# Batch 1's turned u accumulated in PSUM, and the steps of its mixer placed later

## The chip, the core and the metric

The kernel runs on one core of one Trainium2 chip. The metric is the device time of one execution in microseconds. Five runs of the kernel before gave 222.54 to 223.18 us, with a median of 222.9 us. One more look at the same program is a profile, from which all rows below come. TensorE is called PE in the rows, VectorE DVE, ScalarE ACT, GpSimd POOL and the queue of SyncE SP or SPq; PEld is TensorE loading weights.

## What is computed

Four batches of 768 positions and 512 channels (8 heads of 64). First a retention layer, whose output x is the input of a mixer with a low-rank product over positions and an MLP over channels:

```python
for t in range(S):
    state = gamma * state + k[t] (outer) v[t]      # per batch and head
    y[t] = scale * q[t] @ state
x = y as (batch, position, 512)
u = x + (x.T @ U @ V).T                            # U: 768x32, V: 32x768
out = u + relu(u @ w_ch1) @ w_ch2                  # 512 -> 2048 -> 512
```

## The kernel before, in words

**Retention in chunks.** Each batch has 6 chunks of 128 positions, in 3 pairs. For a chunk, `state` (line 482) adds k x v to a running state in one PSUM bank and ScalarE copies it out; `score_one` (521) multiplies turned k by turned q into two "s" banks (line 506), and VectorE screens them with the causal mask (line 516); `mix` (532) multiplies q by the incoming state (line 540) and the screened scores by v (line 545) into the "o" bank, which ScalarE copies to x (line 548). Before that, `prep_keys` (280) scales q and k and casts v on GpSimd, and for batch 1 `turn_pe` (461) turns q and k on TensorE into the one "qk" bank (line 465); ScalarE copies the result out, for q in two steps (`q_order`, 453), for k as kT. For batches 2 and 3 the turns are DMA transposes.

**The mixer.** `lr_open` and `lr_proj` (554, 559) project x by U; the result `pc` is a small tile copied by VectorE. `lr_grow` (571) multiplies it by V into four banks, one for each 128 channels (line 576), and `lr_add` (580) adds these to x in place on VectorE (line 582): the tile x is then the plain u. `lr_expand` (586) is both. The MLP wants u turned, as `uT`. Batch 0 gets its first 512 positions of uT without the plain u: `x_turn` (861) turns x by multiplying it with an identity matrix into four PSUM banks (line 865), four 512-column products of V and pc are accumulated into the same banks (line 929), and ScalarE and VectorE copy them out by turns. Batch 1 has its plain u made first and then turned by TensorE's transposes, in pairs of 128 channels (`lr_turn_pair`, 599, into fp16 "s" banks); batches 2 and 3 use DMA transposes (line 609). The last two chunks of a batch are done at the start of its own MLP (`first`, lines 935 and 945: `lr_expand` and, for batches 0 to 2, `lr_turn_pe` of chunks 4 and 5).

**The MLP and the weave.** `mlp_pieces` (761) gives a list of TensorE pieces with their costs: 16 wide up pieces (512 positions, line 772), 16 narrow ones (256 positions), each with a relu on ScalarE or VectorE, and down pieces. In batch 0 the down product is plain: 24 pieces of four 512-column matmuls (line 823), four to an output chunk, with an addition of u on VectorE at the end of each chunk (line 828). In batches 1 to 3 it takes seven half products in place of eight (`down_pairs`, 652), for which VectorE makes sums of w2 beforehand (`w2_sums`, 632: four subtractions of 512 columns for each two blocks of w2; line 617 is where a `part` runs them).

**What sets the order.** The order is written out by hand. `weave` (837) walks through the pieces of batch b-1's MLP and adds up their costs; every other step (retention of batch b, its turns, its mixer, the w2 sums) has a mark, a share of the MLP's total cost, and is issued before the first piece that reaches it. So a mark's meaning is a place in the instruction queue of each engine, and each engine works through its queue in order. For batch 1 the marks come from a list `at`, one for each chunk:

```python
at = [0.475, 0.58, 0.64, 0.695, 0.75, 0.802]
lag = [0.01, 0.035, 0.065]
...
steps = [(state, at[i] + lag[0]),
         (score_one, at[i] + lag[1] - 0.015 * (i == 5)),
         (mix, at[i] + lag[2] + more)]
```

The total cost of batch 0's MLP in the weave's own units is 41.5, of which the 24 down pieces begin at half.

**Banks.** PSUM has 8 banks here, given out by name: "mlp" has three (four from batch 1's MLP on, when "qk" joins), "s" two, "o", "qk" and "st" one each. A step that takes a bank waits until the last reader of its former content is done.

**Loads.** SP issues all loads in order through a ring of 16 tiles, each refilled when GpSimd has read it. After the last load of batch 2, SP's queue holds that batch's six DMA transposes, the six stores of batch 0 and the loads of batch 3.

Of the kernel before, what the change touches and what calls it, by code (L numbers as in the profile page):

```python
# [11 lines left out]
fp16 = mybir.dt.float16  # L12
# [6 lines left out]
def kernel(  # L19
# [11 lines left out]
    nc = tc.nc  # L31
# [40 lines left out]
    def bank(tag, dtype=fp32):  # L72
        n_bank[0] += 1
        ring = RINGS[tag]
        ring.append(ring.pop(0))
        return psum.tile([P, 2048 // (4 if dtype == fp32 else 2)], dtype,
                         tag=f"bank{ring[-1]}", name=f"{tag}_{n_bank[0]}",
                         bufs=1)

    def four(t):  # L80
        return t.rearrange("p (n m) -> p n m", n=4)

    def evac(eng, dst, src):
        if eng == "A":
            nc.scalar.activation(dst, src, AF.Copy)  # L85
        else:
            nc.vector.tensor_copy(out=dst, in_=src)
# [508 lines left out]
        evac("A", uTs[b][:, ds(j0, 2)].rearrange("p j c t -> p (j c) t"),  # L596
             tp.rearrange("p (n t) -> p n t", t=P))

    def lr_turn_pair(b, c0, eng):
        tp = bank("s", fp16)  # L600
        for c in range(c0, c0 + 2):
            for j in range(NLO):
                nc.tensor.transpose(tp[:, ts(NLO * (c - c0) + j, P)],
                                    us[b][:, j, ts(c, P)], ident16)
        evac(eng, uTs[b][:, :NLO, ds(c0, 2)].rearrange("p j c t -> p c j t"),
             tp.rearrange("p (c j t) -> p c j t", c=2, j=NLO))

    def lr_turn(b, j):
        nc.sync.dma_start_transpose(  # L609
            out=uTs[b][:, ds(j, 2)].rearrange("p j c t -> p (j c) t"),  # L610
# [247 lines left out]

    xT = {}

    def x_turn(c, j0):
        if j0 == 0:
            xT[c] = bank("mlp" if c < 3 else "o")
        for j in range(j0, j0 + 2):
            nc.tensor.matmul(xT[c][:, ts(j, P)], xs[0][:, j, ts(c, P)], ident16,
                             start=(j == 0), stop=False, skip_group_check=True)

    def prep_pair(nm, sc, engs):
        for hh in range(2):
# [55 lines left out]
        x_turn(c, 0)  # L925
        x_turn(c, 2)
    idle_bank[0] = bank("s")
    for c in range(NCB):
        nc.tensor.matmul(xT[c][:, :LO], pcs[0][ds(RK * c, RK)],
                         V4[ds(RK * c, RK), :LO], start=False, stop=True,  # L930
                         skip_group_check=True)
    for c in range(NCB):
        evac("AD"[c % 2], uTs[0][:, :NLO, c], four(xT[c]))
    keep_busy(3)
    first = [part(lr_expand, 0, 4, 2), part(lr_turn_pe, 0, 4),
             part(lr_expand, 0, 0, 4)]
# [4 lines left out]
    for b in range(1, B + 1):  # L941
        tracks = []
        if b > 1:
            old = b - 1 < SEVEN
            first = [part(lr_expand, b - 1, 4, 2, "qk" if old else "st"),
                     part(lr_turn_pe, b - 1, 4, "qk" if old else "o")
                     if b < 3 else part(lr_turn, b - 1, 4)]
            if not old:
                RINGS["mlp"] = [6, 0, 1, 2]
        tracks.append((first, *((0.02, 0.2), (0.02, 0.14), (0.0, 0.06),  # L950
                                (0.0, 0.03))[b - 1]))
        if b < B:
            if b == 1:
                at = [0.475, 0.58, 0.64, 0.695, 0.75, 0.802]
                lag = [0.01, 0.035, 0.065]
                for sc in range(NSC):
                    keys = pair(b, sc)
                    c0, c1 = 2 * sc, 2 * sc + 1
                    if sc:
                        tracks.append(([part(prep_keys, b, keys[:AHEAD])],  # L960
                                       at[c0] - 0.1, 1))
                    tracks.append(([part(prep_keys, b, keys[AHEAD:])],
                                   at[c1] - 0.1, 1))
                    for f, d in ((part(turn_pe, "q", b, sc),
                                  at[c0] - (0.04, 0.03, 0.032)[sc]),
                                 (part(turn_pe, "k", b, sc, (0,)),
                                  at[c0] + (0.0, 0.014, 0.014)[sc]),
                                 (part(turn_pe, "k", b, sc, (1,)), at[c1])):
                        tracks.append(([f], d, d))
                for sc in range(NSC):  # L970
                    tracks.append(([part(prep_keys, 2, pair(2, sc))],
                                   at[-1] - 0.05 + 0.03 * sc, 1))
                for i in range(2 * NSC):
                    tracks.append(([part(turn_dma, "kq"[i % 2], 2, i // 2)],
                                   0.84, 0.84))
                for f, d in zip(w2_sums(0) + w2_sums(2),
                                (0.515, 0.53, 0.55, 0.6, 0.65, 0.685, 0.71,
                                 0.745)):
                    tracks.append(([f], d, d))
            else:  # L980
                at = [(0.205, 0.06)[b - 2] + (0.074, 0.1)[b - 2] * i
                      for i in range(NCK)]
                lag = [0.0, 0.04, 0.1]
                two = [(0.25, 0.395, 0.595), (0.1, 0.27, 0.44)][b - 2]
                if b == 2:
                    for _ in range(RING):
                        feed_one(False)
                    steps = [(0.01 + 0.022 * i, f)
                             for i, f in enumerate(w2_sums(4) + w2_sums(6))]
                    for sc in range(NSC):  # L990
                        steps.append((0.57 + 0.08 * sc,
                                      part(prep_keys, 3, pair(3, sc))))
                        for nm in "kq":
                            if not sc:
                                steps.append((0.64, part(turn_dma, nm, 3, sc)))
                else:
                    steps = [(0.08, part(turn_dma, nm, 3, sc))
                             for sc in (1, 2) for nm in "kq"]
                for d, f in steps:
                    tracks.append(([f], d, d))  # L1000
            if b > 1:
                for sc in range(NSC):
                    d = two[sc] - (0.04, 0.05, 0.08 if b == 2 else 0.05)[sc]
                    tracks.append(([lambda b=b, sc=sc: q_order(
                        b, sc, live["q", b, sc])], d, d))
            for i in range(NCK):
                more = 0.012 if b == 1 and i in (0, 2) else 0.0
                if b == 2 and i > 3:
                    p = two[2] + 0.062 * (i - 4)
                    steps = [(state, p - 0.035), (score_one, p),  # L1010
                             (mix, p + 0.075)]
                elif b > 1:
                    p = two[i // 2]
                    steps = [(state, p + (-0.035, 0.02)[i % 2]),
                             (mix, p + (0.08, 0.12)[i % 2])]
                    if i % 2 == 0:
                        steps.append((score_two, p))
                else:
# [3 lines that stand above are left out]
                for f, d in steps:  # L1022
                    tracks.append(([part(f, b, i)], d, d))
            t = at[-1] + lag[2] if b == 1 else two[-1] + 0.122
            if b == 1:
                tracks += [([part(lr_open, b), part(lr_proj, b)], t + 0.02,
                            t + 0.02),
                           ([part(lr_expand, b, 0, 4)], t + 0.04, t + 0.04),
                           ([part(lr_turn_pair, b, 0, "A"),
                             part(lr_turn_pair, b, 2, "D")], t + 0.08, t + 0.12)]  # L1030
            else:
                for fs, d in (([part(lr_open, b), part(lr_proj, b)],
                                (0.042, 0.03)[b - 2]),
                              ([part(lr_grow, b, 0, 4, "st")], 0.065),
                              ([part(lr_add, b, 0, 4, (0,))], 0.065),
                              ([part(lr_add, b, 0, 4, (1,))], 0.075),
                              ([part(lr_add, b, 0, 4, (2,))], 0.1),
                              ([part(lr_add, b, 0, 4, (3,))], 0.12),
                              ([part(lr_turn, b, 0)], 0.14),
                              ([part(lr_turn, b, 2)], 0.141)):  # L1040
                    tracks.append((fs, t + d, t + d))
        weave(b == 1, mlp_pieces(b - 1), *tracks)
# [29 lines left out]
```

## Time and profile before

| what | before |
|---|---|
| median of 5 runs | 222.9 us |
| the profiled execution, its own time | 222.68 us |
| its span, first to last instruction | 220.9 us |
| TensorE busy, share of the span | 212.0 us, 96% |
| VectorE busy | 140.0 us, 63% |
| ScalarE busy | 92.9 us, 42% |
| GpSimd busy | 81.9 us, 37% |
| the first up piece of batch 0's MLP starts | 28.32 us |
| its first down piece starts | 51.31 us |
| the first up piece of batch 1's MLP starts | 84.54 us |
| the first up piece of batch 2's MLP starts | 132.66 us |
| GpSimd's last conversion for batch 2 ends | 87.43 us |

How to read it: the span is what the profile's rows cover, and 1.8 us of the execution's own time lie around it. Matmuls are pipelined, so the rows of TensorE overlap, and the time that a step costs is read from the start of its row to the start of the next one. A row's bracket at its end tells how long the engine stood idle before it and which instruction released it.

### The profile page before, as it was taken

The page shows a single profiled execution, that of the slowest core. Times are in us where ns is not written, and L with a number is a line of the kernel's source. Part 1 is how long each engine was busy: PE and PEld are TensorE (multiplying, and loading weights), DVE is VectorE, ACT ScalarE, POOL GpSimd, SP SyncE. Part 2 cuts the span into 40 slices and gives each one's busy share as a digit, 9 for nine tenths or more (in the row PEclk, how much of TensorE's full clock was granted, in tenths as well). Part 3 has the DMA queues.
Part 4 walks back from the last instruction along what each step waited for, and adds up shares of the span by engine and source line. Part 5 has one row for each costly group of instructions (what it writes and reads, how often), then busy time and mean ns, then how long its engine had stood idle before and what let it go on. Part 6 is the DMA issues. An engine that isn't in the chain of part 4 may idle for free. (4 is left out here: it accounts for less than half of the span.)

```text
span 220.9 us, 5513 instructions
## 1 busy us (share of the span) xinstructions
PE 212.0 (96%) x2235; PEld 148.1 (67%) x2235; DVE 140.0 (63%) x302; ACT 92.9 (42%) x191; POOL 81.9 (37%) x121
## 2 busy tenths in 40 slices
PE   7979999999998999999999989999999999999994
PEld 2768754596554554667788774767788856668884
DVE  7478666235554558599686854598977442867443
ACT  3357654475556214676911005768510035551000
POOL 5456868986987868000059930000000000000000
PEclk9999999999999999999999999999999999999999
DMA  5999999999999999999999578900003541000043
GB/s 163 301 292 268 235 358 283 369 363 217 237 238 233 243 223 223 184 331 252 231 231 178 169 166 189 123 1 3 0 3 71 190 145 24 3 1 0 10 160 119
DMA packets 84489, 38.82 MB, mean 176 GB/s; under 512 B 58384, under 2 KB 77552, under 8 KB 84464
## 3 DMA queue, kind: packets, MB, share of 16 engines
q1 hardware_dynamic: 83456, 36.84, 69.9%
q10 hardware_dynamic: 1008, 1.64, 2.1%
q8 instruction: 17, 0.28, 0.6%
q14 instruction: 8, 0.07, 0.1%
HBM read 27.46 MB, written 6.29 MB: 153 GB/s over the span
## 5 line engine op out<-in xcount | busy, mean ns | idle before, releaser
L772 PE MATMUL mlp<-uT,w1b 128*128 128x512 f16 (+1 forms) x512 | 88.9, 326 | 0.8 <-DMA uT<-x 0.8
L782 ACT ACTIVATE gT<-mlp 128x512 f16<-128x512 f32 (+1 forms) x98 | 47.2, 490 | 61.9 <-PE mlp L772 59.8
L772 PEld LDWEIGHTS <-w1b 128*128 128x128 f16 x512 | 48.2, 98 | 30.9 <-issue 1.1
L780 DVE TENSOR_SCALAR gT<-mlp 128x512 f16<-128x512 f32 (+1 forms) x30 | 16.7, 557 | 28.5 <-PE mlp L772 27.9
L664 PEld LDWEIGHTS <-gT 128*128 128x128 f16 x288 | 27.7, 98 | 3.3
L823 PE MATMUL mlp<-w2b,gT 128*128 128x512 f16 x96 | 24.2, 380 | 0.0
L516 DVE TENSOR_TENSOR a<-s,mask 128x512 bf16<-128x512 f32 x26 | 16.7, 683 | 8.3 <-PE s L506 8.2
L306 POOL TENSOR_TENSOR kd<-in,gk 128x512 bf16<-128x512 f32 x18 | 19.4, 1088 | 5.5 <-DMA in<-in_k_dram 4.9
L664 PEld LDWEIGHTS <-gS 128*128 128x128 f16 x200 | 19.2, 98 | 2.6
L85 ACT ACTIVATE x<-o 128x512 f16<-128x512 f32 x20 | 11.9, 596 | 17.5 <-PE o L545 17.1
L306 POOL TENSOR_TENSOR qd<-in,gq 128x512 bf16<-128x512 f32 x18 | 18.8, 1063 | 0.0
L664 PE MATMUL A<-w2t,gT 128*128 128x256 f16 x144 | 18.4, 273 | 0.0
L85 ACT ACTIVATE state<-st 64x256 bf16<-64x256 f32 x40 | 15.0, 375 | 7.3 <-PE st L490 3.5
L823 PEld LDWEIGHTS <-gT 128*128 128x128 f16 x96 | 8.2, 98 | 7.2
L304 POOL CAST vd<-in 128x512 bf16<-128x512 f32 x18 | 10.9, 618 | 1.7 <-DMA in<-in_v_dram 1.2
L340 POOL CAST w1b<-in 128x512 f16<-128x512 f32 x16 | 9.7, 613 | 2.8 <-DMA in<-in_moe_w_ch_dram 2.3
L346 POOL CAST w2b<-in 128x512 f16<-128x512 f32 x16 | 9.6, 614 | 1.5 <-DMA in<-in_moe_w_ch_dram 0.8
L617 POOL COPY gate<-gT 128x1 f16<-128x1 f16 x1 | 0.2, 190 | 25.4 <-DVE gT L617 25.4
L664 PE MATMUL B<-w2b,gT 128*128 128x256 f16 x72 | 9.3, 273 | 0.0
L582 DVE TENSOR_TENSOR x<-s,x 128x256 f16<-128x256 f32 (+1 forms) x16 | 8.1, 548 | 1.2 <-issue 0.7
L664 PE MATMUL A<-w2t,gS 128*128 128x256 f16 x72 | 8.9, 273 | 0.0
L664 PE MATMUL A<-w2b,gT 128*128 128x256 f16 x72 | 8.8, 272 | 0.0
(151 smaller groups left out, 288.5 us busy)
## 6 DMA issues: line engine op xcount, KB each, us to landing
in<-in_moe_w_ch_dram SPq DMA_DIRECT2D x32, 256.0 KB, 5.5
in<-in_k_dram SPq DMA_DIRECT2D x24, 256.0 KB, 5.5
in<-in_q_dram SPq DMA_DIRECT2D x24, 256.0 KB, 4.7
in<-in_v_dram SPq DMA_DIRECT2D x24, 256.0 KB, 5.3
out_dram<-o SPq DMA_DIRECT2D x16, 256.0 KB, 2.3
out_dram<-o ACTq DMA_DIRECT2D x6, 256.0 KB, 2.1
out_dram<-o SPq DMA_DIRECT2D x3, 128.0 KB, 1.7
Uf<-in_moe_U_dram SPq DMA_DIRECT2D x1, 96.0 KB, 5.9
```

The lines of the kernel that those rows point to most:

```text
L85: nc.scalar.activation(dst, src, AF.Copy)
L304: nc.gpsimd.tensor_copy(out=t, in_=src)
L306: nc.gpsimd.tensor_tensor(t, src, g, op=ALU.mult)
L340: nc.gpsimd.tensor_copy(out=w1b[:, c, ts(mb, 512)], in_=take("w1", mb, c))
L346: nc.gpsimd.tensor_copy(out=w2b[:, m], in_=take("w2", m))
L516: nc.vector.tensor_tensor(a, four(sp[i]), causal(mask), op=ALU.mult)
L582: nc.vector.tensor_tensor(us[b][:, ds(j0, nj), ts(c, P)], four(grown[b][c])[:, :nj], xs[b][:, ds(j0, nj), ts(c, P)], op=ALU.add)
L664: nc.tensor.matmul(acc[key, i], lhs[:, m, ts(i, P)], rhs[:, m], start=(fresh and m == 0), stop=(m == NH - 1), skip_group_check=True)
L772: nc.tensor.matmul(g_p[:, :sz], w1b[:, c, ts(m, P)], uTs[b][:, ds(j, nj), c], start=(c == 0), stop=(c == NCB - 1))
L780: nc.vector.tensor_relu(gT[:, m, ds(lo, sz)], g_p[:, :sz])
L782: nc.scalar.activation(gT[:, m, ds(lo, sz)], g_p[:, :sz], AF.Relu)
L823: nc.tensor.matmul(ch, gT[:, m, ts(j, P)], w2b[:, m], start=(m == 0), stop=(m == NM - 1))
```

## The change

- Batch 1's first 512 positions are turned as batch 0's are: `x_turn` now takes a batch and a bank, and the four-product part with its copies is a function, `grow_turned`. The four banks are "qk", "st" and both "s". The first two are turned before the projection, the other two behind it. `lr_turn_pair` is gone, and so is the making of batch 1's plain u for these positions in MLP 0.
- That plain u is made in MLP 1 instead: its 16 products (`lr_grow`) at 0.1 of that MLP, its four VectorE additions (`lr_add`) at 0.1 to 0.166.
- The w2 sums of blocks 4 and 5 (and of their partners 12 and 13), four VectorE subtractions, move from MLP 1 to MLP 0, and the other eight there get other places.
- The list `at` of batch 1 is later by 0.015 to 0.033; the q turns lie 0.042 ahead of their chunk, the k turns of a pair's first chunk at its mark. The marks for preparing batch 2's k, q and v stay where they were.
- GpSimd's and SP's queues hold the same instructions in the same order as before. TensorE has 4 more matmuls.

```diff
@@ -596,15 +596,6 @@
         evac("A", uTs[b][:, ds(j0, 2)].rearrange("p j c t -> p (j c) t"),
              tp.rearrange("p (n t) -> p n t", t=P))
 
-    def lr_turn_pair(b, c0, eng):
-        tp = bank("s", fp16)
-        for c in range(c0, c0 + 2):
-            for j in range(NLO):
-                nc.tensor.transpose(tp[:, ts(NLO * (c - c0) + j, P)],
-                                    us[b][:, j, ts(c, P)], ident16)
-        evac(eng, uTs[b][:, :NLO, ds(c0, 2)].rearrange("p j c t -> p c j t"),
-             tp.rearrange("p (c j t) -> p c j t", c=2, j=NLO))
-
     def lr_turn(b, j):
         nc.sync.dma_start_transpose(
             out=uTs[b][:, ds(j, 2)].rearrange("p j c t -> p (j c) t"),
@@ -858,12 +849,20 @@
 
     xT = {}
 
-    def x_turn(c, j0):
+    def x_turn(c, j0, b=0, tag=None):
         if j0 == 0:
-            xT[c] = bank("mlp" if c < 3 else "o")
+            xT[c] = bank(tag or ("mlp" if c < 3 else "o"))
         for j in range(j0, j0 + 2):
-            nc.tensor.matmul(xT[c][:, ts(j, P)], xs[0][:, j, ts(c, P)], ident16,
+            nc.tensor.matmul(xT[c][:, ts(j, P)], xs[b][:, j, ts(c, P)], ident16,
                              start=(j == 0), stop=False, skip_group_check=True)
+
+    def grow_turned(b):
+        for c in range(NCB):
+            nc.tensor.matmul(xT[c][:, :LO], pcs[b][ds(RK * c, RK)],
+                             V4[ds(RK * c, RK), :LO], start=False, stop=True,
+                             skip_group_check=True)
+        for c in range(NCB):
+            evac("AD"[c % 2], uTs[b][:, :NLO, c], four(xT[c]))
 
     def prep_pair(nm, sc, engs):
         for hh in range(2):
@@ -925,12 +924,7 @@
         x_turn(c, 0)
         x_turn(c, 2)
     idle_bank[0] = bank("s")
-    for c in range(NCB):
-        nc.tensor.matmul(xT[c][:, :LO], pcs[0][ds(RK * c, RK)],
-                         V4[ds(RK * c, RK), :LO], start=False, stop=True,
-                         skip_group_check=True)
-    for c in range(NCB):
-        evac("AD"[c % 2], uTs[0][:, :NLO, c], four(xT[c]))
+    grow_turned(0)
     keep_busy(3)
     first = [part(lr_expand, 0, 4, 2), part(lr_turn_pe, 0, 4),
              part(lr_expand, 0, 0, 4)]
@@ -951,7 +945,7 @@
                                 (0.0, 0.03))[b - 1]))
         if b < B:
             if b == 1:
-                at = [0.475, 0.58, 0.64, 0.695, 0.75, 0.802]
+                at = [0.49, 0.6, 0.665, 0.725, 0.783, 0.835]
                 lag = [0.01, 0.035, 0.065]
                 for sc in range(NSC):
                     keys = pair(b, sc)
@@ -962,20 +956,20 @@
                     tracks.append(([part(prep_keys, b, keys[AHEAD:])],
                                    at[c1] - 0.1, 1))
                     for f, d in ((part(turn_pe, "q", b, sc),
-                                  at[c0] - (0.04, 0.03, 0.032)[sc]),
+                                  at[c0] - 0.042),
                                  (part(turn_pe, "k", b, sc, (0,)),
-                                  at[c0] + (0.0, 0.014, 0.014)[sc]),
+                                  at[c0]),
                                  (part(turn_pe, "k", b, sc, (1,)), at[c1])):
                         tracks.append(([f], d, d))
                 for sc in range(NSC):
                     tracks.append(([part(prep_keys, 2, pair(2, sc))],
-                                   at[-1] - 0.05 + 0.03 * sc, 1))
+                                   0.752 + 0.03 * sc, 1))
                 for i in range(2 * NSC):
                     tracks.append(([part(turn_dma, "kq"[i % 2], 2, i // 2)],
                                    0.84, 0.84))
-                for f, d in zip(w2_sums(0) + w2_sums(2),
-                                (0.515, 0.53, 0.55, 0.6, 0.65, 0.685, 0.71,
-                                 0.745)):
+                for f, d in zip(w2_sums(0) + w2_sums(2) + w2_sums(4),
+                                (0.53, 0.545, 0.56, 0.59, 0.64, 0.655, 0.71,
+                                 0.725, 0.765, 0.79, 0.865, 0.885)):
                     tracks.append(([f], d, d))
             else:
                 at = [(0.205, 0.06)[b - 2] + (0.074, 0.1)[b - 2] * i
@@ -986,7 +980,10 @@
                     for _ in range(RING):
                         feed_one(False)
                     steps = [(0.01 + 0.022 * i, f)
-                             for i, f in enumerate(w2_sums(4) + w2_sums(6))]
+                             for i, f in enumerate(w2_sums(6))]
+                    steps.append((0.1, part(lr_grow, 1, 0, 4, "st")))
+                    steps += [(0.1 + 0.022 * c, part(lr_add, 1, 0, 4, (c,)))
+                              for c in range(NCB)]
                     for sc in range(NSC):
                         steps.append((0.57 + 0.08 * sc,
                                       part(prep_keys, 3, pair(3, sc))))
@@ -1023,11 +1020,14 @@
                     tracks.append(([part(f, b, i)], d, d))
             t = at[-1] + lag[2] if b == 1 else two[-1] + 0.122
             if b == 1:
-                tracks += [([part(lr_open, b), part(lr_proj, b)], t + 0.02,
-                            t + 0.02),
-                           ([part(lr_expand, b, 0, 4)], t + 0.04, t + 0.04),
-                           ([part(lr_turn_pair, b, 0, "A"),
-                             part(lr_turn_pair, b, 2, "D")], t + 0.08, t + 0.12)]
+                turns = [part(x_turn, c, j0, b, tag)
+                         for c, tag in enumerate(("qk", "st", "s", "s"))
+                         for j0 in (0, 2)]
+                for fs, d in ((turns[:4], t + 0.006),
+                              ([part(lr_open, b), part(lr_proj, b)], t + 0.022),
+                              (turns[4:], t + 0.023),
+                              ([part(grow_turned, b)], t + 0.044)):
+                    tracks.append((fs, d, d))
             else:
                 for fs, d in (([part(lr_open, b), part(lr_proj, b)],
                                 (0.042, 0.03)[b - 2]),
```

## The prediction

> **What bounds the kernel now.** I read the page first, then the chain of waits, then TensorE's timeline from 27 us to 139 us, adding up what each step should take and looking for the steps that took longer.
>
> ```profile
> PE   7979999999998999999999989999999999999994
> PEclk9999999999999999999999999999999999999999
> ...
> PE 39%; DMA 2%; SPq 1%; DVE 0%; issue 0%
> ```
>
> TensorE is busy in every slice at full clock and carries the chain that ended last (the two small shares, DMA and SP's queue, are one wait at batch 2's turn). So this is a TensorE-order kernel: its time changes by TensorE work added or taken away, and by the holes in its queue. The other engines count only where they make such a hole. The holes of the first MLP, where the change works, are seen in TensorE's timeline:
>
> ```profile
> 57.61 0.27 PE L465 MATMUL qk<-ident,qd 128*128 128x128 bf16 x2
> 58.33 0.51 PE L465 MATMUL qk<-ident,qd 128*128 128x128 bf16 x6 [0.45 <-POOL qd L306]
> ...
> 60.20 0.64 PE L545 MATMUL o<-vd,a 128*128 128x64 bf16 x8
> 60.67 1.03 PE L823 MATMUL mlp<-w2b,gT 128*128 128x512 f16 x4
> ...
> 61.98 1.03 PE L823 MATMUL mlp<-w2b,gT 128*128 128x512 f16 x4
> 63.41 0.40 PE L506 MATMUL s<-qO,kT 64*128 64x128 bf16 x8 [0.41 <-ACT kT L85]
> ...
> 69.24 0.29 PE L545 MATMUL o<-vd,a 128*128 128x64 bf16 x4
> 69.84 0.29 PE L545 MATMUL o<-vd,a 128*128 128x64 bf16 x4 [0.31 <-DVE a L516]
> 69.97 0.39 PE L490 MATMUL st<-vd,kd 128*128 128x128 bf16 x4
> ...
> 70.41 1.03 PE L823 MATMUL mlp<-w2b,gT 128*128 128x512 f16 x4
> 72.10 0.40 PE L506 MATMUL s<-qO,kT 64*128 64x128 bf16 x8 [0.66 <-ACT kT L85]
> ```
>
> Ends overlap in these rows, so I go from start to start. Undisturbed prices, from neighbouring rows: a down piece (4 matmuls) 0.87, a wide up piece 0.87, a narrow one 0.44, a q turn 0.45, a k turn or state step 0.22, a score step 0.33, a mix 0.23 (first) or 0.45, and 0.09 more when tiles change from 128 rows to 64 or 32. Against these the holes are:
> - q turn of pair 1: 57.61 to 58.77 = 1.16, less 0.44: 0.72, for POOL's q.
> - mix 1: 0.47, less 0.23: 0.24 (no releaser printed; its screens started at 59.20 and took 1.29).
> - score 2: 1.43 before it, less 0.96: 0.47, for ScalarE's kT.
> - mix 3: 0.73, less 0.23: 0.50, for VectorE's screen.
> - score 4: 1.69, less 0.96: 0.73, for ScalarE's kT.
>
> Together 2.66 us. From 75 us to batch 2's turn at 131 us I find no hole.
>
> **The change part by part.**
>
> *TensorE's work for batch 1's u.* Out go 16 products L576 (0.33) and 16 transposes (L603, 0.45 per 8 from 81.92 to 82.37, so 0.90). In come 16 identity matmuls and four 512-column products; the same code for batch 0 shows both: 8 in 0.45 (26.48 to 26.93), and 27.25 to 27.58 = 0.33 for the four. So the tail of MLP 0 costs TensorE the same, with the same two tile switches. The plain u's 16 products come again in MLP 1: +0.33, +0.09 for a switch = **+0.42**.
> Here a rule has to be weighed. The Trainium skill ("TensorE: Matmul & The Clock Gate", Part 4: PE-mode transpose) puts a 128x128 transpose at about 275 ns in a kernel and says that the clock does not rise for it. Taken as issue time, swapping 16 transposes for matmuls would then be worth 16 x (275 - 56) ns = 3.5 us. The rows contradict that: L603 transposes and L865 identity matmuls both last 219 ns and follow each other every 56 ns at granted clock 1.00. I take the rows: the swap is worth nothing.
>
> *The chain at the end of MLP 0.* Before: projection 78.43, products 79.85, four VectorE additions 80.56 to 83.0, transposes, two copies of 1.02 and 0.69, up at 84.54, all hidden under down pieces. After: turned x, projection, grown product, four copies, two on each engine. By batch 0's rows from the grown product to the last copy's end it is 29.00 - 27.25 = 1.75. Two down pieces and the product itself make 0.33 + 1.74 = 2.07 before the up pieces, so it is hidden by 0.3; without one of these pieces it would cost 0.55. The chain is shorter, and that is what lets all steps be placed about 0.03 of the MLP later; by itself it saves nothing.
>
> *The steps moved.* I lay the new order on the old timeline. Narrow up pieces begin at 43.46. Twelve of them instead of ten bring the first q turn to 48.67 (was 47.80). Its copies qO on ScalarE end 2.0 after its start as before (48.44 + 1.34 against 47.80), at 50.65; the relu of the next piece is queued behind them until 50.9, and the fourth piece needs its bank (at 50.42). That is a new hole of 0.5; the first down piece is then at 51.6 (was 51.31). Behind it queue kT and the first score, all of TensorE's.
> This hole costs nothing, for the q turn of pair 1 keeps its place behind six down pieces. It would start at 58.1 and must wait for POOL's q, whose second half begins on TensorE at 58.33. It ends at 58.77 as before, POOL being fed by DMA and its queue, like SP's, keeping its order. Without that cover the 0.5 would be paid in full.
> From 58.77 on: a down piece now precedes score 1 (59.73), and down piece and k turn lie between score and mix. Mix 1 starts 61.15; its second screen is ready at 60.06 + 1.39 = 61.45 and used at 61.49: hole gone. Score 2 is at 63.66; its kT was turned at 60.93 and copied by 61.9, with no qO and no state copy in front: gone. q turn 2 is at 66.16 (q ready at 64.66). Score 3 is at 68.02, its screen done at 69.74, used at 69.78 in mix 3: gone, by 0.04. Its o bank needs x(2), behind two state copies and two qO copies, about 69.0; mix 3 starts 69.44. Score 4 is at 71.93, its kT turned at 69.22 and ready by 70.2: gone. Mix 4 starts 73.35, but screen 4 stands behind an output addition (71.95 to 72.6): ready 73.85, wanted 73.69: a new **0.2**. Score 5 at 75.0, mix 5 at 77.1, turned x at 77.5, projection at 78.9, grown product at 80.8, MLP 1 at about 82.8 against 84.54.
> As a sum: 0.24 + 0.47 + 0.50 + 0.73 = 1.94 removed, 0.2 new: **-1.74**.
>
> *VectorE's load.* Four w2 differences leave MLP 1 for MLP 0 (0.42 each, 1.7), four additions (0.68 each, 2.6) go the other way. The first lie in VectorE's idle time before scores, except for what POOL does to them. The skill speaks against placing them there: "GPSIMD Engine Reference", section 1, Specifications, says that POOL's SBUF interfaces are shared and contended by VectorE instructions with two SBUF inputs, as these are. The rows: 14 of 16 at 0.41 to 0.44, but 1.13 at 56.24 and 1.06 at 85.35, under POOL's q, and POOL's 2.04 us pairs stretched to 2.2 to 2.3. By the rule all four are slowed: +0.7 each on VectorE, and POOL's q for pair 1 could come 0.2 later, on the path. By most rows it is nothing. A gain is excluded, for nothing of this load leaves POOL's busy time. I take 0 and keep +0.2.
>
> *The plain u in MLP 1.* Its products stand one up piece behind the turn of the last two chunks, and want bank o, which ScalarE must empty first. In the rows of before:
>
> ```profile
> 88.32 0.61 PE L594 MATMUL o<-ident,x 128*128 128x128 f16 x8
> ...
> 88.97 1.02 ACT L85 ACTIVATE uT<-o 128x1024 f16<-128x1024 f16 x1 [0.71 <-PE o L594]
> ```
>
> From turn to empty bank 1.67; turn, one piece and switch take 0.45 + 0.87 + 0.09 = 1.41: a new wait of 0.26, say **+0.3** with the semaphore. Nothing in the trace has this wait; bounds 0 (a gain is excluded, since products were not there) and 1.0 (a relu in front of the copy, 0.6 more). Behind it stand the up pieces, and ScalarE and VectorE waiting for these; all shift together. The four additions end some 0.3 before the state step of batch 2 wants bank st.
>
> *The rest.* The wait at 132.66 (0.79) follows TensorE's own projection by a fixed chain and moves with it. From there nothing changes.
>
> Sum: -1.74 + 0.42 + 0.3 = **-1.0 us**. The profiled execution took 222.68 (span 220.9), so 221.7; the median of the runs is 222.9, so **221.9**.
>
> **The rivals.**
> - *The holes only move (wash).* ScalarE's queue around 66 to 69 us holds 0.77 + 1.34 + 0.60 of copies and I left 0.4 before mix 3; mix 3's screen has 0.04. Against it: the long gaps from k turn to score. If two of the four holes come back (mean 0.49), -1.0 + 0.97: about 222.8.
> - *Slower: ScalarE's queue hands its wait on.* Place: the kT copies ahead of scores 2 and 4. If a kT copy waits behind qO, state and x copies still, all of the 1.94 stays and 0.72 of MLP 1 is added: 223.6. It decides from kT being ready more than 1.7 us later than I have it (scores at 63.66 and 71.93 against copies ending 61.9 and 70.2). The unhurried ScalarE queue (idle 1.68 before kT at 65.04) speaks against it.
> - *More than I say.* Bank o is empty in time and mix 4 waits not: -1.0 - 0.5, and q of pair 1 arriving 0.2 earlier: about 221.2.
> - *That the stalls belonged to data, not order:* POOL's q at 58.27 is the only one, and I keep it.
>
> **How the numbers follow.** My forecast 0.60 (221.4 to 222.4), the larger gain 0.10, the wash 0.16, slower 0.14. A measurement here can tell about 0.2% (0.45 us) from no change. Faster by more: 0.60 + 0.10 = 0.70; the wash 0.16; slower 0.14. The range 221.2 to 223.0 takes in forecast, wash and half of the larger gain, with +0.2 for POOL and +0.7 for bank o inside it.
>
> **What would show it.** MLP 1's first up product near 82.8, no wait for kT, the q turn of pair 1 still waiting for POOL until about 58.3, a hole of 0.5 before it for ScalarE, one of 0.2 at mix 4, one of 0.3 before the plain u's products. I am wrong if scores 2 and 4 or mix 3 still wait, if q of pair 1 is later than 58.5, or if the up pieces of MLP 1 wait for a uT copy.

## The result and the profile after

The changed kernel takes 222.05 us, the median of 43 runs (221.40 to 222.68), the kernel before 222.4 us (80 runs, 221.62 to 223.37; its first five had given 222.9). The ratio is 0.9982 with a 95% interval of 0.9975 to 0.9990, so the change saves 0.4 us (0.2 to 0.6), where 1.0 was forecast, with a chance of 0.70 for a gain above 0.45. The profiled execution took 222.24 us with a span of 220.5.

In the changed kernel's line numbers L763 is an up piece, L814 a down piece of MLP 0, L771 and L773 are relus, and L608 stands for the w2 sums (L617 before). On its page, TensorE and its clock look as before, and TensorE carries 92% of the chain that ended last (in the kernel before, the chain began at the wait for batch 2's turn, at 126 us):

```profile
PE   7989999999999999999999989999999999999994
PEclk9999999999999999999999999999999999999999
...
PE 92%; DVE 3%; ACT 3%; issue 1%; ACTq 0%
```

TensorE's timeline at the places of the old holes (columns: start, duration, engine, line, operation, operands, count, and in brackets the idle time before it):

```profile
49.84 1.47 PE L763 MATMUL mlp<-uT,w1b 128*128 128x256 f16 x12
51.67 0.60 PE L763 MATMUL mlp<-uT,w1b 128*128 128x256 f16 x4 [0.35 <-ACT gT L773]
...
58.84 0.61 PE L465 MATMUL qk<-ident,qd 128*128 128x128 bf16 x8
59.29 1.03 PE L814 MATMUL mlp<-w2b,gT 128*128 128x512 f16 x4
...
61.90 0.42 PE L545 MATMUL o<-vd,a 128*128 128x64 bf16 x8
62.15 1.03 PE L814 MATMUL mlp<-w2b,gT 128*128 128x512 f16 x4
63.02 0.39 PE L490 MATMUL st<-vd,kd 128*128 128x128 bf16 x4
63.24 1.03 PE L814 MATMUL mlp<-w2b,gT 128*128 128x512 f16 x4
64.20 0.40 PE L506 MATMUL s<-qO,kT 64*128 64x128 bf16 x8
...
70.23 0.42 PE L545 MATMUL o<-vd,a 128*128 128x64 bf16 x8
70.48 1.03 PE L814 MATMUL mlp<-w2b,gT 128*128 128x512 f16 x4
71.34 0.39 PE L490 MATMUL st<-vd,kd 128*128 128x128 bf16 x4
71.57 1.03 PE L814 MATMUL mlp<-w2b,gT 128*128 128x512 f16 x4
72.53 0.40 PE L506 MATMUL s<-qO,kT 64*128 64x128 bf16 x8
...
74.18 0.69 PE L545 MATMUL o<-vd,a 128*128 128x64 bf16 x8
74.70 1.03 PE L814 MATMUL mlp<-w2b,gT 128*128 128x512 f16 x4
```

Mixes 1 and 3 now take 0.25 from start to start, and scores 2 and 4 follow their down piece after 0.96: the four holes are gone. New are the hole before the piece at 51.67 (1.83 for three pieces worth 1.31: 0.52) and that of mix 4 (0.52 less 0.23: 0.29). One thing is not as forecast: the q turn of pair 1 at 58.84 doesn't wait for POOL; it takes 0.45.

In MLP 1 the plain u's products stop for bank o, which ScalarE empties (its copy ends at 88.97):

```profile
87.30 0.61 PE L594 MATMUL o<-ident,x 128*128 128x128 f16 x8
87.75 1.03 PE L763 MATMUL mlp<-uT,w1b 128*128 128x512 f16 x4
87.95 1.02 ACT L85 ACTIVATE uT<-o 128x1024 f16<-128x1024 f16 x1 [0.71 <-PE o L594]
88.71 0.23 PE L576 MATMUL s<-pc,V 32*128 32x128 f16 x2
89.03 0.21 PE L576 MATMUL o<-pc,V 32*128 32x128 f16 x1
```

From the first product at 88.71 to the first that writes bank o at 89.03 are 0.32 us.

For comparing profiles I measure stages by the starts of TensorE's rows: "opening" is the start of the first up piece of MLP 0, "MLP 0" runs from there to the first up piece of MLP 1, "up 1" from there to its first down piece, and "q turn" is how long the q turn of pair 1 waited: what it took beyond 0.44, or beyond 0.53 where a score follows it (before, c0, e4, e8), since the change to tiles of 64 rows costs 0.09.

| kernel | opening | MLP 0 | up 1 | q turn | median of runs | ratio to before |
|---|---|---|---|---|---|---|
| before | 28.32 | 56.22 | 25.53 | 0.63 | 222.4 | 1 |
| changed | 29.05 | 54.47 | 26.28 | 0.0 | 222.05 | 0.9982 (0.9975 to 0.9990) |
| before, second profile (c0) | 28.88 | 56.06 | 25.54 | 0.47 | one run, 222.97 | |
| e1, q turn 0 at nine pieces | 28.52 | 54.68 | 26.28 | 0.22 | 221.90 | 0.9979 (0.9967 to 0.9991) |
| e2, plain u later | 28.32 | 54.78 | 26.45 | 0.15 | 221.88 | 0.9977 (0.9964 to 0.9989) |
| e3, e1 + e2 + score 4 | 28.47 | 54.19 | 26.45 | 0.0 | 221.67 | 0.9974 (0.9961 to 0.9986) |
| e4, new turn alone | 28.66 | 55.59 | 26.51 | 0.0 | 223.43 | 1.0049 (1.0030 to 1.0068) |
| e5, mlp bank | 29.39 | 54.47 | 25.97 | 0.0 | 221.62 | 0.9961 (0.9943 to 0.9979) |
| e6, q turn 0 at ten pieces | 28.43 | 54.13 | 26.28 | 0.0 | 221.36 | 0.9949 (0.9930 to 0.9968) |
| e7, e5 + e6 + score 4 | 28.39 | 53.75 | 25.97 | 0.0 | 221.15 | 0.9939 (0.9920 to 0.9957) |
| e8, before with k turns first | 28.10 | 55.58 | 25.53 | 0.91 | 220.87 | 0.9932 (0.9910 to 0.9955) |
| e9, w2 sums late | 28.57 | 54.47 | 26.51 | 0.0 | 222.09 | 0.9991 (0.9973 to 1.0010) |
| e10, e8 with scores earlier | 28.84 | 53.64 | 25.54 | 0.0 | 220.28 | 0.9901 (0.9870 to 0.9932) |
| e11, e10 with the new turn | 28.95 | 54.37 | 26.47 | 0.76 | 220.99 | 0.9938 (0.9915 to 0.9961) |

From MLP 2's first up piece to the end of the span, all take 88.20 to 88.30 us. The opening, whose order of work is the same in all, starts MLP 0 anywhere from 28.10 to 29.39. So one profile's span says little here: from MLP 0's first up piece to the end, the changed kernel's profile is 1.13 us shorter than that of before (191.45 against 192.58), its span only 0.4, its opening having been 0.73 later.

### The profile page after: what moved, and what is told of

Read it like the earlier page. It is cut to its first block, busy times and chain, and to the rows that moved or that the text cites. A ratio compares the mean times of both kernels' runs of the same rounds, so it can differ in the third digit from the quotient of the medians.

```text
span 220.5 us, 5522 instructions
## 1 busy us (share of the span) xinstructions
PE 213.1 (97%) x2239; PEld 148.0 (67%) x2239; DVE 143.6 (65%) x303; ACT 93.0 (42%) x192; POOL 81.7 (37%) x121
## 4 chain that ended last, share of the span: by engine, by line
PE 92%; DVE 3%; ACT 3%; issue 1%; ACTq 0%
PE mlp L763 37%; PE A L655 14%; PE mlp L814 9%; PE C L655 6%; PE B L655 4%; PE mlp L189 3%; PE o L545 2%; PE s L506 2%; ACT qT L85 2%; PE st L490 2%; PE o L540 1%; PE qk L465 1%; PE mlp L363 1%; DVE a L413 1%; PE s L576 1%; PE mlp L193 1%
## 5 line engine op out<-in xcount | busy, mean ns | idle before, releaser
L763 PE MATMUL mlp<-uT,w1b 128*128 128x512 f16 (+1 forms) x512 | 88.9, 326 | 0.9 <-DVE x L582 0.6
L773 ACT ACTIVATE gT<-mlp 128x512 f16<-128x512 f32 (+1 forms) x98 | 47.3, 490 | 63.0 <-PE mlp L763 60.8
L763 PEld LDWEIGHTS <-w1b 128*128 128x128 f16 x512 | 48.1, 98 | 31.2 <-issue 1.3
L771 DVE TENSOR_SCALAR gT<-mlp 128x512 f16<-128x512 f32 (+1 forms) x30 | 16.7, 557 | 27.6 <-PE mlp L763 27.1
L814 PE MATMUL mlp<-w2b,gT 128*128 128x512 f16 x96 | 24.2, 380 | 0.0
L814 PEld LDWEIGHTS <-gT 128*128 128x128 f16 x96 | 8.1, 98 | 7.2 <-issue 0.2
L304 POOL CAST vd<-in 128x512 bf16<-128x512 f32 x18 | 11.9, 672 | 0.7 <-DMA in<-in_v_dram 0.5
L608 POOL COPY gate<-gT 128x1 f16<-128x1 f16 x1 | 0.2, 190 | 26.6 <-DVE gT L608 26.6
L340 POOL CAST w1b<-in 128x512 f16<-128x512 f32 x16 | 9.0, 611 | 0.1
```

What stands on the lines that cost most here:

```text
L304: nc.gpsimd.tensor_copy(out=t, in_=src)
L340: nc.gpsimd.tensor_copy(out=w1b[:, c, ts(mb, 512)], in_=take("w1", mb, c))
L763: nc.tensor.matmul(g_p[:, :sz], w1b[:, c, ts(m, P)], uTs[b][:, ds(j, nj), c], start=(c == 0), stop=(c == NCB - 1))
L771: nc.vector.tensor_relu(gT[:, m, ds(lo, sz)], g_p[:, :sz])
L773: nc.scalar.activation(gT[:, m, ds(lo, sz)], g_p[:, :sz], AF.Relu)
L814: nc.tensor.matmul(ch, gT[:, m, ts(j, P)], w2b[:, m], start=(m == 0), stop=(m == NM - 1))
```

## The experiments

Each ratio above is to runs of the kernel before that were taken together with it.

**e1: the first q turn earlier.**

```diff
-                                  at[c0] - 0.042),
+                                  at[c0] - (0.063, 0.042, 0.042)[sc]),
```

> The changed kernel with the q turn of batch 1's pair 0 two narrow up pieces earlier (ten up pieces before it, as before the change), so that ScalarE's two qO copies no longer stand before a relu whose bank TensorE wants next: the hole of 0.52 us at 51.67 us of the changed kernel's profile goes. Theory A (the hole is paid: in most executions the q turn of pair 1 does not wait for POOL, so nothing behind the hole takes it in): 0.5 us less than the changed kernel, about 0.9 us less than before, and no wait of the q turn of pair 1 in the profile. Theory B (the hole is hidden by POOL's q, as I forecast, and the missing gain is lost elsewhere): same time as the changed kernel, 0.4 us less than before, and the q turn of pair 1 waits for POOL by some 0.5 us.

221.90 us, no clear gain, and it doesn't decide between the theories: the mark fell at nine narrow pieces, not ten, and the hole stayed. The fourth piece behind the q turn still waited for a relu (1.83 for three pieces worth 1.31):

```profile
47.55 0.61 PE L465 MATMUL qk<-ident,qd 128*128 128x128 bf16 x8
48.00 1.47 PE L763 MATMUL mlp<-uT,w1b 128*128 128x256 f16 x12
49.83 1.91 PE L763 MATMUL mlp<-uT,w1b 128*128 128x256 f16 x16 [0.35 <-ACT gT L773]
```

Every third relu is VectorE's and there are three mlp banks, so nine and twelve pieces give the same pattern: the first piece behind the q turn has its relu on ScalarE, behind the two qO copies (1.34 us), and the fourth piece needs that piece's bank.

**e2: the plain u later.**

```diff
-                    steps.append((0.1, part(lr_grow, 1, 0, 4, "st")))
-                    steps += [(0.1 + 0.022 * c, part(lr_add, 1, 0, 4, (c,)))
+                    steps.append((0.13, part(lr_grow, 1, 0, 4, "st")))
+                    steps += [(0.13 + 0.022 * c, part(lr_add, 1, 0, 4, (c,)))
```

> The changed kernel with the plain u's products and additions in MLP 1 later by 0.03 of that MLP, so that TensorE has one more up piece between the turn into bank o and the product that wants this bank. Theory A (the wait of 0.32 us at 88.71 us for ScalarE's copy is on the path): 0.3 us less than the changed kernel, 0.7 less than before. Rival (the wait only moves, to the state step of batch 2 that wants bank st from the last addition, or to a relu bank held up by VectorE's additions): no gain, and a hole of about 0.3 us before 94 us in its profile.

221.88 us. The rival was right in the profile: the products run through, but the state step of batch 2 waits for VectorE's last addition, and up 1 takes 26.45 instead of 26.28. (The difference of 0.17 us in the medians is inside the intervals.)

```profile
93.45 0.38 PE L490 MATMUL st<-vd,kd 128*128 128x128 bf16 x4 [0.32 <-DVE x L582]
```

**e3: both, and the score of chunk 4 earlier.**

```diff
-                             (score_one, at[i] + lag[1] - 0.015 * (i == 5)),
+                             (score_one, at[i] + lag[1] - (0.0, 0.0, 0.0, 0.0, 0.007, 0.015)[i]),
```

> Both of these edits, and the score of chunk 4 earlier by 0.007 of the MLP, so that VectorE screens it ahead of the output addition of chunk 3 and mix 4 need not wait (0.29 us at 74.18 us). If all three holes are paid: 0.5 + 0.3 + 0.3 = 1.1 us less than the changed kernel, 1.5 less than before, about 220.9. If POOL's q hides the first: 0.6 less than the changed kernel. If the time is set elsewhere (by the loads of batch 0 and the order behind 96 us): about the same as the changed kernel.

221.67 us. Only the third edit worked: mix 4's hole is gone (0.24 from start to start) and MLP 0 is 0.28 shorter. The median is 0.4 below the changed kernel's, with intervals that overlap.

**e4: the new turn alone.** The changed kernel with the marks of before:

```diff
-                at = [0.49, 0.6, 0.665, 0.725, 0.783, 0.835]
+                at = [0.475, 0.58, 0.64, 0.695, 0.75, 0.802]
-                                  at[c0] - 0.042),
+                                  at[c0] - (0.04, 0.03, 0.032)[sc]),
-                                  at[c0]),
+                                  at[c0] + (0.0, 0.014, 0.014)[sc]),
-                for f, d in zip(w2_sums(0) + w2_sums(2) + w2_sums(4),
-                                (0.53, 0.545, 0.56, 0.59, 0.64, 0.655, 0.71,
-                                 0.725, 0.765, 0.79, 0.865, 0.885)):
+                for f, d in zip(w2_sums(0) + w2_sums(2),
+                                (0.515, 0.53, 0.55, 0.6, 0.65, 0.685, 0.71,
+                                 0.745)):
-                             for i, f in enumerate(w2_sums(6))]
+                             for i, f in enumerate(w2_sums(4) + w2_sums(6))]
```

> The new way of turning batch 1's u and the plain u made in MLP 1, with all marks of batch 1, of its q and k turns and of the w2 sums as in the kernel before. By my sum the new way saves nothing itself and adds 0.33 + 0.09 of products and 0.3 of waiting in MLP 1: 0.7 us more than before (ratio 1.003). Rival (the shorter chain at the end of MLP 0 saves time by itself): not slower than before.

223.43 us, 1.04 more than before (0.7 to 1.5). The rival falls: with these marks the shorter chain saves nothing. The holes of before are back (0.41 and 0.67 for kT, 0.31 for a screen), and up 1 takes 26.51. TensorE's order is that of before up to the end of MLP 0's retention, yet the q turn of pair 1 did not wait for POOL, whose conversions of that q ended at 57.39 here and at 58.27 in the profile of before. First the row of before, then those of e4:

```profile
56.05 2.22 POOL L306 TENSOR_TENSOR qd<-in,gq 128x512 bf16<-128x512 f32 x2
...
54.98 2.41 POOL L306 TENSOR_TENSOR qd<-in,gq 128x512 bf16<-128x512 f32 x2
57.94 0.61 PE L465 MATMUL qk<-ident,qd 128*128 128x128 bf16 x8
58.48 0.40 PE L506 MATMUL s<-qO,kT 64*128 64x128 bf16 x8
```

Its MLP 0 is 0.63 shorter than that of before, which is just the wait. From e4 to the changed kernel, which has the same turn of u with the later marks and the moved sums, the medians fall by 1.38.

**e5: the last turn into an mlp bank.**

```diff
-                     part(lr_turn_pe, b - 1, 4, "qk" if old else "o")
+                     part(lr_turn_pe, b - 1, 4, "qk" if old else "mlp" if b == 2 else "o")
```

> The changed kernel with batch 1's last two chunks turned into an mlp bank in place of bank o, so that the plain u's products of MLP 1 need not wait for ScalarE's copy and keep their place. Theory A (the 0.32 us of waiting are on the path): MLP 1's up phase 25.95 us from its first up piece to its first down piece, against 26.28 in the changed kernel's profile, and 0.3 us less time. Rival (the state step's wait for VectorE's last addition into bank st, seen when the products were placed later, takes its place): 26.2 to 26.4, no gain.

221.62 us, a median 0.4 below the changed kernel's (the intervals overlap by a little); up 1 takes 25.97, as theory A said. The wait for bank o was on the path of this stage; with its cause taken away nothing waits in its place, while moving the step (e2) only moved the wait.

**e6: ten pieces before the first q turn.**

```diff
-                                  at[c0] - 0.042),
+                                  at[c0] - (0.053, 0.042, 0.042)[sc]),
```

> The changed kernel with exactly ten narrow up pieces before the first q turn (nine keep the hole, since every third relu is VectorE's and the same relu falls behind the qO copies). Now the hole of 0.52 us must go from the profile. Theory A (it is paid in most executions): MLP 0 takes 54.0 us from its first up piece, or 54.2 where the q turn of pair 1 waits for POOL a little; 0.3 to 0.5 us less time than the changed kernel, 221.6. Theory B (POOL's q hides it): MLP 0 54.5, the q turn of pair 1 waits 0.5 us for POOL, no gain.

221.36 us, 0.7 less than the changed kernel, and the two intervals do not overlap. Most of the hole is gone, and no wait for POOL takes its place:

```profile
47.91 0.61 PE L465 MATMUL qk<-ident,qd 128*128 128x128 bf16 x8
48.35 2.86 PE L763 MATMUL mlp<-uT,w1b 128*128 128x256 f16 x24
51.05 0.39 PE L465 MATMUL qk<-ident,kd 128*128 128x128 bf16 x4
...
57.80 0.61 PE L465 MATMUL qk<-ident,qd 128*128 128x128 bf16 x8
58.24 1.03 PE L814 MATMUL mlp<-w2b,gT 128*128 128x512 f16 x4
```

Six pieces take 2.70 where 2.61 is their price, and the q turn of pair 1 takes 0.44. Theory A holds: the hole was paid. In the profile MLP 0 is 0.34 shorter than the changed kernel's (54.13 against 54.47), not 0.52: 0.09 of the hole is left, and mix 1 takes 0.34 in place of 0.25. The 0.7 of the medians is more than that, but the intervals leave room for 0.2 to 1.3.

**e7: all three holes of the change closed**, by the edits of e5, e6 and the score of e3:

```diff
-                                  at[c0] - 0.042),
+                                  at[c0] - (0.053, 0.042, 0.042)[sc]),
-                             (score_one, at[i] + lag[1] - 0.015 * (i == 5)),
+                             (score_one, at[i] + lag[1] - (0.0, 0.0, 0.0, 0.0, 0.007, 0.015)[i]),
-                     part(lr_turn_pe, b - 1, 4, "qk" if old else "o")
+                     part(lr_turn_pe, b - 1, 4, "qk" if old else "mlp" if b == 2 else "o")
```

> Ten pieces before the first q turn, the mlp bank, and the earlier score of chunk 4: all three holes that the change opened. If they are paid: MLP 0 53.7, MLP 1's up phase 25.95, together 1.1 us less than the changed kernel, about 221.0. With the first hidden by POOL's q and the second moved to the state step: 0.3 less, 221.7.

221.15 us, ratio 0.9939. MLP 0 takes 53.75 and up 1 25.97 as expected, and between the opening and batch 2's turn TensorE's list of waits is empty. The remaining 0.44 of up 1 over before is the plain u's products and a tile switch (0.42 forecast).

**e8: the kernel before, with the k turns first in their place.**

```diff
-                                  at[c0] + (0.0, 0.014, 0.014)[sc]),
+                                  at[c0] + (0.0, 0.0095, 0.001)[sc]),
```

> The kernel before the change, with only this: the k turns of pairs 1 and 2 stand ahead of the state step (pair 1), and of the mix and state steps (pair 2), of the same place in the order, not behind them, so that ScalarE copies kT before the state and x copies. Batch 1's u is turned as before. If the two waits for kT (0.47 and 0.73 us) were the main cost and no other wait takes them up: 1.2 us less than before, 221.2, and less than the changed kernel, which pays 0.75 us in MLP 1. If the gain of the change hangs on the new turn of u: about as before.

220.87 us, ratio 0.9932: 1.67 less than before in its runs (1.0 to 2.0), where 1.2 was expected, and less than the changed kernel. Before, ScalarE had copied x, state and then kT (71.45 to 72.05, with score 4 waiting until 72.10). Now kT comes first, and score 4 finds it ready:

```profile
69.51 0.60 ACT L85 ACTIVATE kT<-qk 128x512 bf16<-128x512 bf16 x1 [0.99 <-PE qk L465]
70.26 0.60 ACT L85 ACTIVATE x<-o 128x512 f16<-128x512 f32 x1
70.75 0.77 ACT L85 ACTIVATE state<-st 64x256 bf16<-64x256 f32 x2
```

```profile
70.28 1.03 PE L823 MATMUL mlp<-w2b,gT 128*128 128x512 f16 x4
71.24 0.40 PE L506 MATMUL s<-qO,kT 64*128 64x128 bf16 x8
```

The score starts 0.96 behind its down piece, so no hole is left there. Neither later marks nor the new turn of u are needed for that. (This one execution had the longest wait for POOL's q of all, 0.91, and lost 0.36 before its first q turn as well; without the two its MLP 0 of 55.58 would be 54.31. Its own time, 221.65, is the highest of the six runs.)

**c0: the kernel before, profiled again**, unchanged.

> The kernel before, unchanged, for a second profile of it. If my account of the lost gain holds (the profile I read had a q turn of pair 1 that waited 0.72 us for POOL, which most executions of the kernel before don't have): MLP 0 takes 55.5 us from its first up piece to the first of MLP 1, against 56.22, and the q turn of pair 1 does not wait. If the wait is usual: 56.2 again.

MLP 0 takes 56.06, and the q turn waits again, a little less:

```profile
58.16 0.28 PE L465 MATMUL qk<-ident,qd 128*128 128x128 bf16 x2
58.73 0.51 PE L465 MATMUL qk<-ident,qd 128*128 128x128 bf16 x6 [0.29 <-POOL qd L306]
```

The wait is 0.47 after 0.63. That is a miss for my account in its strong form: two profiles of two have the wait. Both executions (222.68 and 222.97) are slower than the median of 222.4, and e4, with the same order up to here, has no wait; how often the wait occurs can't be read from these alone.

**e9: the w2 sums of blocks 4 and 5 left in MLP 1.**

```diff
-                for f, d in zip(w2_sums(0) + w2_sums(2) + w2_sums(4),
+                for f, d in zip(w2_sums(0) + w2_sums(2),
...
-                             for i, f in enumerate(w2_sums(6))]
+                             for i, f in enumerate(w2_sums(4) + w2_sums(6))]
```

> The changed kernel with the w2 sums of blocks 4 and 5 left in MLP 1 as before. If four more subtractions under POOL's work slow it where TensorE feels it: 0.2 us or more faster than the changed kernel, and POOL's q of pair 1 earlier. If VectorE takes them in idle time: no gain, rather 0.2 us more, since the eight sums and the additions of u then crowd VectorE before the state step of batch 2. My account: as the changed kernel or slower, 222.0 to 222.4.

222.09 us, the changed kernel's time within the intervals. MLP 0 takes 54.47 in both, so the four sums cost TensorE nothing there. Up 1 takes 26.51 in place of 26.28, for with all eight sums and the additions in MLP 1 the state step of batch 2 waits for VectorE, as the second account expected; 0.23 us is too little to show in these medians.

**e10: e8 with two scores earlier.**

```diff
-                             (score_one, at[i] + lag[1] - 0.015 * (i == 5)),
+                             (score_one, at[i] + lag[1] - (0.0, 0.006, 0.0, 0.002, 0.0, 0.015)[i]),
```

> The kernel before with the k turns first (220.87 us, 1.67 less than before in its runs), and also the score of chunk 1 ahead of the q turn of pair 1, and the score of chunk 3 one down piece earlier, ahead of the output addition of chunk 2 on VectorE: the holes at mix 1 (0.25) and mix 3 (0.30) go, and the first score fills some of the wait for POOL's q. 0.5 to 0.8 us less than the k turns alone: 220.1 to 220.4, MLP 0 in 54.1 us or less from its first up piece. If the holes are taken up by other waits: 220.9.

220.28 us, ratio 0.9901, the fastest of all. MLP 0 takes 53.64. Mixes 1 and 3 have no hole (0.23 each). Score 1 now stands ahead of the q turn; what that place is worth this profile doesn't show, for POOL's q was ready at 58.11, before score 1 began:

```profile
58.23 0.40 PE L506 MATMUL s<-qO,kT 64*128 64x128 bf16 x8
58.55 0.62 PE L465 MATMUL qk<-ident,qd 128*128 128x128 bf16 x8
59.01 1.03 PE L823 MATMUL mlp<-w2b,gT 128*128 128x512 f16 x4
...
60.10 0.40 PE L545 MATMUL o<-vd,a 128*128 128x64 bf16 x8
60.33 1.03 PE L823 MATMUL mlp<-w2b,gT 128*128 128x512 f16 x4
...
68.63 0.40 PE L545 MATMUL o<-vd,a 128*128 128x64 bf16 x8
68.86 0.39 PE L490 MATMUL st<-vd,kd 128*128 128x128 bf16 x4
```

**e11: e10 with the new turn of u**, written as edits of e4:

```diff
-                                  at[c0] + (0.0, 0.014, 0.014)[sc]),
+                                  at[c0] + (0.0, 0.0095, 0.001)[sc]),
-                             (score_one, at[i] + lag[1] - 0.015 * (i == 5)),
+                             (score_one, at[i] + lag[1] - (0.0, 0.006, 0.0, 0.002, 0.0, 0.015)[i]),
-                     part(lr_turn_pe, b - 1, 4, "qk" if old else "o")
+                     part(lr_turn_pe, b - 1, 4, "qk" if old else "mlp" if b == 2 else "o")
```

> The kernel with the k turns and the two scores placed earlier (220.28 us, 1.99 less than before in its runs), and on top of it the new way of turning batch 1's u: turned x and grown product in PSUM, the plain u made in MLP 1, with the mlp bank for the last turn and all w2 sums where the kernel before has them. In this order TensorE has no hole that a shorter chain could help. My account (the new turn saves no time of its own and costs its products once more): MLP 0 as without it, 53.6 us from its first up piece, MLP 1's up phase 26.0 to 26.2 in place of 25.53, 0.5 to 0.7 us more, 220.8 to 221.0. Rival (the shorter chain at the end of MLP 0 is worth something): as fast or faster, 220.3 or less.

220.99 us: 0.7 more than e10, as my account said, though their intervals overlap a little. Up 1 takes 26.47: VectorE, with all eight sums there, holds the state step by 0.33. The profile's MLP 0 of 54.37 contains a wait for POOL of 0.76; without it, it is that of e10.

## Why the prediction was right in sign and too large

*What bounds the kernel* was right: the time moved with the holes in TensorE's queue and its added work, and nothing behind batch 2's turn changed but for the wait there (0.79 us before, 0.60 in the changed kernel).

*The four holes removed (1.94)* were right, each at its place; scores 2 and 4 were forecast for 63.66 and 71.93 and came at 64.20 and 72.53, with an MLP 0 that began 0.73 later. Mix 4 cost 0.29 where 0.2 was said.

*MLP 1 (+0.42 and +0.3)* was right: up 1 grew by 0.75. e5 and e7 split it into 0.31 for the bank and 0.44 for the products.

*The new turn of u is worth nothing itself*: right (e4, e11). In the changed kernel, too, 8 identity matmuls took 0.46 from start to start.

*The step that failed* is "This hole costs nothing, for the q turn of pair 1 keeps its place behind six down pieces". Size and cause of the hole were right (0.5 said, 0.52 seen), and so was the place of the q turn (58.84 with an opening 0.73 later, which is 58.11 on the old timeline; 58.1 was said). Its cover was not. I took POOL's arrival at 58.33 in one execution for a fixed time. Counted from MLP 0's first up piece and without the tile change, the q turn ended at 30.36 and 30.19 us in the two profiles of before and at 29.73 in e4. With the hole in the order it ended at 30.24 to 30.45 (six profiles, the latest two after a short wait for POOL), without it at 29.81 (e6, e7). So the hole sets a floor of 30.24, and it replaced the wait for POOL instead of hiding under it: where POOL is in time, the hole is paid in full.

With the hole paid, the measured parts give -1.94 + 0.52 + 0.29 + 0.75 = -0.38. Stages in which POOL was in time give the same: MLP 0 takes 54.47 in the changed kernel and 55.59 in e4, as in before without its wait, and up 1 is 0.75 longer than before, together -0.37. Measured were -0.4 (-0.2 to -0.6). The median of e4, too, lies 1.04 above that of before, where up 1 accounts for 0.98: this fits a kernel before that rarely waits.

*An agreement that is luck.* MLP 0 is 1.75 shorter in the changed kernel's profile than in that of before, where the forecast had 1.74. But 0.63 of it is the wait for POOL in that one execution of before, which the forecast kept. The absolute number, 221.9, was near by luck too: it was counted from 222.9, which was high for the kernel before.

*What stays open* is how often POOL's q is late. Up to that q GpSimd converts the same tiles in the same order in all 14 profiles, and it was done 28.51 to 30.74 us behind MLP 0's first up piece. The order of before wants it by 29.3, and in nine of the 14 it came later; the order with the hole wants it by 29.8, and in five it came later. If these arrivals hold for both orders, the wait is 0.39 us on average in the first and 0.15 in the second (an estimate). The hole would then cost about half its price, and the change would save 0.6, at the outer edge of the measured interval (0.56). The runs speak rather for the hole paid in full, but don't settle it.

*Slips in the working.* The 0.72 of the q turn holds 0.09 of tile change by the prediction's own prices, and the place of score 1 (59.73) counts that change again. Four additions of 0.68 are 2.7, not 2.6. Neither moves the answer by more than 0.1.

*VectorE under POOL.* I took "most rows" (0.42 each) over the rule of the Trainium skill ("GPSIMD Engine Reference", section 1, Specifications: contended interfaces for VectorE instructions with two SBUF inputs). In the main the rule was right: over the 14 profiles, 107 of the 119 sums that lay wholly within POOL's work took more than 0.43, and none of the 55 outside it. The view of the tile w2t gives ns min/median/max, first before, then in the changed kernel:

```profile
L617 DVE TENSOR_TENSOR w2t<-w2b x8: 410/418/1056, 53.9 to 90.3; 128x512 f16<-128x512 f16 x8
L617 DVE TENSOR_TENSOR w2t<-w2b,w2t x8: 406/420/1127, 54.4 to 93.0; 128x512 f16<-128x512 f16 x8
...
L608 DVE TENSOR_TENSOR w2t<-w2b x8: 412/655/825, 56.0 to 86.6; 128x512 f16<-128x512 f16 x8
L608 DVE TENSOR_TENSOR w2t<-w2b,w2t x8: 409/658/1079, 56.8 to 88.1; 128x512 f16<-128x512 f16 x8
```

The medians rose from 418 and 420 to 655 and 658, and the last four sums of MLP 0 took 0.71 to 1.08 us each. TensorE felt nothing of the four in MLP 0, as e9 shows, so the 0 in the sum stands for another reason than I gave: VectorE had the time. "A gain is excluded" was wrong, if by little: with them gone MLP 1's up phase was spared 0.23.

*The rival "slower"* (kT handed on in ScalarE's queue) did not come: scores 2 and 4 have no wait.

## What to carry to other kernels

A hole that one profile shows to be covered by a late arrival is covered only in the executions in which it is late: price it in full, or put other work there. Where a wait names an engine's copy, look first at what stands ahead of that copy in the same place of the order: moving two turns ahead of state steps (e8) won about four times what the whole change did. And if a step waits for a bank, give it another bank before moving it, since a moved step may make the next one wait (e2).

## What the runs showed of the hardware

VectorE's fp16 subtractions of two SBUF tensors of 128x512 took 0.41 to 0.43 us with POOL idle and up to 1.31 us with POOL at work (e7); in the changed kernel POOL's casts rose from 0.61 to 0.80 under them and its scalings from 1.04 to 1.22. The opening of the same instructions, fed by loads, ended anywhere from 28.10 to 29.39 us, a spread three times the effect measured here.
